# Two decode layers on one core: the last head of each pass loaded and worked off in another order

## The chip, the core and the metric

The kernel runs on one core of one Trainium2 chip. The metric is the device time of one execution in microseconds. Three runs of the kernel before gave 1331.91, 1332.23 and 1334.55 us, the median being 1332.23 us.

A profiled execution records when each engine worked. TensorE does the matrix products (PE in the rows, PEld its loads of stationary operands), VectorE is DVE, ScalarE is ACT, GpSimd is POOL, and SyncE (SP) issues the loads from HBM. "x16" counts trace records; each float32 product of the code is two records (two passes) in these rows.

## What is computed

Two layers, each of them attention and then a gated feed-forward part, run twice over the same weights and the same caches, for 2 batches and one new token each:

```python
def _A_ref(x, k_cache, v_cache, wq, wo):
    B, Sq, D = x.shape                 # 2, 1, 448
    H, Dh = 16, 256
    q = (x @ wq).reshape(B, Sq, H, Dh).transpose(0, 2, 1, 3)
    scores = jnp.einsum("bhqd,bhkd->bhqk", q, k_cache) * (Dh ** -0.5)   # 4096 keys
    o = jnp.einsum("bhqk,bhkd->bhqd", softmax(scores), v_cache)
    return o.transpose(0, 2, 1, 3).reshape(B, Sq, H * Dh) @ wo

def _B_ref(x, W_gate, W_up, W_down):   # 448 -> 1792 -> 448
    gate, up = x @ W_gate, x @ W_up
    return (gate * (gate > 0) * up) @ W_down

for _ in range(2):
    x = x + _A_ref(layernorm(x), A_k_cache, A_v_cache, A_wq, A_wo)
    x = x + _B_ref(layernorm(x), B_W_gate, B_W_up, B_W_down)
```

All of it is float32. Keys and values of one head and batch are 4 MB each, so that a pass over 32 of these pairs reads 256 MB.

## The kernel before, in words

**Units.** A unit is one pair of head and batch. A pass works through 32 units; the second pass takes them in the reverse order. `attention` keeps `n_u = 32`, and unit 31 is the last of a pass, unit 30 the one before it (both of one head).

**The arena.** All loads go into one big on-chip buffer, `arena`, of 27 places of 1 MB: six blocks of four places and three singles. `pending` is the list of all loads of the program in their order, written before any instruction. `pump()` takes loads from its front as long as there is a free place, and issues each on SP's queue; `release()` frees a place after its last use and calls `pump()` again. Keys or values of a unit are loaded as one piece of 4 MB, which needs a whole free block, or as four pieces of 1 MB. `grouped(keys, begin, end)` decides: the first `begin` and the last `end` pieces of a pass's list stay single. Each load on SP waits for the place's last reader, and, since eight semaphores are used in turn, for the landing of the load eight places earlier.

**Order of the loads.** For each unit its keys and then its values, with the next head's weights between; after unit 31 come seven pieces of the feed-forward input weights (`in`, 0.9 MB each) and four of the output weights (`out`). `keep` holds the pieces that the second pass will need first (22 pieces of keys and values and one head's weights): at the end of the first pass they stay in the arena and are not loaded again, which leaves four places for the eleven feed-forward pieces to pass through.

**A unit.** `score(u, c)` multiplies the query with a quarter of the keys into the PSUM banks `rawa` and `rawb` (L327). `score_copy` (DVE, L337) copies a bank to `found_s` or `row`, `score_turn` (L345) turns it by products with an identity. `softmax_max` and `softmax_exp` use DVE, POOL and ACT. `weigh(u, c)` (L382) multiplies the probabilities with a quarter of the values into `poa` or `pob`, two columns of probabilities against 512 columns, so that half of each result is used. `out_copy` (ACT, L395) and `out_add` (DVE, L398) bring the two useful halves together in `row`; `out_turn` (L406), `out_keep` (DVE, L415) and `project` (L245, through `add`) multiply with the output weights into `y`. These last three of unit u-1 stand between the scores of unit u. `query(u)` (L303, L306) makes the two queries of a head.

**Fillers.** `busy(n, half)` (L236) issues products whose result nobody reads, between the steps of units 30 and 31 and in the feed-forward part.

**Feed-forward.** `absorb()` (L250 to L261) takes the sum in `y` out and turns it, centred, into `xs`; `squares`, `deviation` (L281, L282) and `inverse` give one over the deviation; `again()` (L267) puts the residual back into `y`. `proj(0, ...)` and `proj(1, ...)` (L480) multiply `xs` with the `in` pieces, four and four parts, and release a piece after its last part. `hid` is formed (L504, L506), turned (L511, L516), and multiplied with 14 blocks of the `out` pieces (L245): even blocks go to partitions 0 and 32 of `y`, odd ones to 64 and 96. In the last feed-forward part only, the blocks after 6 all go to partitions 0 and 32, the upper half of `y` is copied to SBUF (L537) and added by two products (L541), so that one copy (L556) yields the output.

## Time and profile before

| | us |
|---|---|
| median of 3 runs | 1332.23 |
| the profiled execution | 1334.14 |
| its span, first to last instruction | 1332.3 |
| PE busy in the span | 1039.9 |
| DVE, ACT, POOL busy | 176.8, 91.7, 47.7 |
| read from HBM | 561.52 MB, 421 GB/s over the span |

Rows of the timeline read: start, duration, engine, line, operation, what it writes and reads, count, and in brackets the idle time of that engine just before and what ended it. Rows of the table by stretches read: stretch, its length, busy time of PE, PEld, DVE, ACT and POOL with counts, the granted share of the TensorE clock, the busy share of the DMA engines, and GB/s moved. A row on SP is the issue of a load, not the load.

### The profile page before, as it was taken

Reading aid. Unit: us, or ns where it says so; the run is one execution under the profiler, and the core shown is the slowest. Engines: PE = TensorE matmul, PEld = TensorE weight load, DVE = VectorE, ACT = ScalarE, POOL = GpSimd, SP = SyncE. Lnnn points to the kernel's source line nnn. Section 1 sums busy time; section 2 is a strip of 40 time slices with the busy share of each in tenths; the row PEclk is TensorE's granted clock in tenths of the full one; section 3 lists DMA queues with packets and bytes.
Section 4 is the critical chain, followed back from the end, with each engine's and each line's share of the span. In section 5 each row is a group of like instructions: output and inputs, shape, how many; then the busy total and the mean of one; then the engine's idle time right before and its main releaser. Section 6 shows DMA issues by size and latency. Waiting matters only on the chain.

```text
span 1332.3 us, 14966 instructions
## 1 busy us (share of the span) xinstructions
PE 1039.9 (78%) x6594; PEld 401.6 (30%) x6594; DVE 176.8 (13%) x522; ACT 91.7 (7%) x280; POOL 47.7 (4%) x134
## 2 busy tenths in 40 slices
PE   4876878787777877768889888787877777677888
PEld 2332222233232323223343333233232232222323
DVE  1111111111011111111101111111111111111110
ACT  1000000000000000000011000000000000000001
POOL 0000000000000000000000000000000000000000
PEclk9868667767677667776888887766667777777689
DMA  9999999999999999999989999999999999999997
GB/s 402 435 426 431 432 422 438 427 433 428 427 434 432 427 431 430 430 431 425 419 333 387 435 432 429 431 429 430 430 430 429 431 430 428 428 434 430 428 418 302
DMA packets 29598, 562.49 MB, mean 422 GB/s; under 512 B 3287, under 2 KB 3421, under 8 KB 10205
## 3 DMA queue, kind: packets, MB, share of 16 engines
q1 hardware_dynamic: 29524, 561.53, 98.8%
q8 instruction: 52, 0.85, 0.3%
q14 instruction: 14, 0.11, 0.0%
q10 hardware_dynamic: 8, 0.01, 0.0%
HBM read 561.52 MB, written 0.00 MB: 421 GB/s over the span
## 4 chain that ended last, share of the span: by engine, by line
PE 66%; DMA 15%; another core or an unknown queue 12%; DVE 3%; issue 2%; ACT 2%; POOL 1%; POOLq 0%; SPq 0%; ACTq 0%; DVEq 0%
PE pob L382 12%; PE poa L382 11%; PE rawa L327 11%; PE rawb L327 11%; PE small L345 11%; DMA arena<-in_k_cache_dram 7%; DMA arena<-in_v_cache_dram 5%; PE pq L303 3%; PE small L406 3%; DMA arena<-in_w_in_dram 2%; DVE row L337 2%; PE y L245 2%; PE pq L306 1%; ACT probs L362 1%
## 5 line engine op out<-in xcount | busy, mean ns | idle before, releaser
L327 PE MATMUL rawa<-arena,q 128*1 128x512 f32 x1024 | 172.1, 785 | 131.3 <-DMA arena<-in_k_cache_dram 130.9
L382 PE MATMUL pob<-arena,probs 128*2 128x512 f32 x1024 | 182.3, 866 | 53.6 <-DMA arena<-in_v_cache_dram 53.1
L382 PE MATMUL poa<-arena,probs 128*2 128x512 f32 x1024 | 177.5, 846 | 52.5 <-ACT probs L362 46.7
L327 PE MATMUL rawb<-arena,q 128*1 128x512 f32 x1024 | 169.7, 737 | 0.0
L345 PE MATMUL small<-ident,row 128*128 128x4 f32 x512 | 83.1, 286 | 30.3 <-DVE row L337 30.3
L345 PEld LDWEIGHTS small<-ident,row 128*128 128x128 f32 x512 | 77.5, 232 | 85.2 <-DVE row L337 85.2
L345 PEld LDWEIGHTS small<-ident,found_s 128*128 128x128 f32 x512 | 79.0, 236 | 71.4 <-issue 37.7
L327 PEld LDWEIGHTS rawa<-arena,q 128*1 128x1 f32 x1024 | 26.8, 91 | 241.3 <-issue 189.9
L345 PE MATMUL small<-ident,found_s 128*128 128x4 f32 x512 | 84.6, 289 | 0.0
L382 PEld LDWEIGHTS pob<-arena,probs 128*2 128x2 f32 x1024 | 30.6, 108 | 173.1 <-issue 170.1
L382 PEld LDWEIGHTS poa<-arena,probs 128*2 128x2 f32 x1024 | 29.6, 106 | 168.8 <-issue 117.2
L337 DVE COPY found_s<-rawa 128x512 f32<-128x512 f32 x64 | 44.2, 691 | 233.0 <-PE rawa L327 233.0
L337 DVE COPY row<-rawb 128x512 f32<-128x512 f32 x64 | 44.3, 691 | 228.6 <-PE rawb L327 228.6
L359 ACT ACTIVATE nm<-top,nsr 128x1 f32<-128x1 f32 x64 | 18.8, 294 | 733.4 <-POOL top L354 733.4
L406 PEld LDWEIGHTS small<-ones,row 128*128 128x128 f32 x256 | 42.9, 238 | 77.9 <-issue 53.8
L354 POOL PARTITION_ALL_REDUCE top<-mx x64 | 22.4, 351 | 1180.1 <-DVE mx L352 1180.1
L303 PE MATMUL pq<-xs,arena 128*128 128x2 f32 x384 | 57.9, 267 | 0.5 <-DVE xs L261 0.5
L303 PEld LDWEIGHTS pq<-xs,arena 128*128 128x128 f32 x384 | 54.3, 213 | 0.7 <-DVE xs L261 0.7
L406 PE MATMUL small<-ones,row 128*128 128x1 f32 x256 | 48.3, 293 | 0.5 <-DVE row L398 0.5
L398 DVE SCALAR_TENSOR_TENSOR row<-pob,ri,row 128x256 f32<-128x256 f32 x32 | 15.5, 484 | 230.9 <-ACT row L395 230.9
L398 DVE SCALAR_TENSOR_TENSOR row<-poa,ri,row 128x256 f32<-128x256 f32 x32 | 15.5, 484 | 168.2 <-ACT row L395 168.2
L395 ACT ACTIVATE row<-pob,ri 128x256 f32<-128x256 f32 x32 | 15.1, 473 | 250.8 <-PE pob L382 250.8
(80 smaller groups left out, 363.0 us busy)
## 6 DMA issues: line engine op xcount, KB each, us to landing
arena<-in_k_cache_dram SPq DMA_DIRECT2D x57, 4096.0 KB, 54.0
arena<-in_v_cache_dram SPq DMA_DIRECT2D x56, 4096.0 KB, 54.1
arena<-in_w_head_dram SPq DMA_DIRECT2D x31, 896.0 KB, 52.4
arena<-in_v_cache_dram SPq DMA_DIRECT2D x22, 1024.0 KB, 19.8
arena<-in_k_cache_dram SPq DMA_DIRECT2D x16, 1024.0 KB, 18.0
arena<-in_w_in_dram SPq DMA_DIRECT2D x14, 896.0 KB, 19.0
arena<-in_w_out_dram SPq DMA_DIRECT2D x4, 896.0 KB, 12.3
arena<-in_w_out_dram SPq DMA_DIRECT2D x3, 672.0 KB, 7.0
```

Of the source, the lines that this page charges most:

```text
L245: nc.tensor.matmul(y[at : at + B, : w_h.shape[1]], stat, w_h, **flags)
L303: nc.tensor.matmul(pq[:, j, :], w[:, at : at + P], xT[:, c, :], start=(c == 0), stop=False)
L306: nc.tensor.matmul(pq[:, j, :], w[:, FULL * DH : FULL * DH + P], xT[:, FULL + j, :], start=False, stop=True,)
L327: nc.tensor.matmul(raw[half][32 * g : 32 * g + 1, :], q_of[u][:, j, :], kt[:, g, :], start=(j == 0), stop=(j == 1),)
L337: nc.vector.tensor_copy(row if half else found_s, raw[half])
L345: nc.tensor.matmul(s_of[u][:, n : n + G], rows[:, e * P : (e + 1) * P], pick, start=True, stop=True,)
L354: nc.gpsimd.partition_all_reduce(mx_of[u], mx, P, RED.max)
L359: nc.scalar.activation(nm, mx_of.pop(u), AF.Copy, scale=nsr[:, b : b + 1])
L382: nc.tensor.matmul(po_of[u][32 * t : 32 * t + 2, :], p_of[u][:, n : n + 2], vt[:, 2 * t * DH : (2 * t + 2) * DH], start=(c == 0), stop=(c ...
L395: nc.scalar.activation(row[:, :DH], po_of[u][:, :DH], AF.Copy, scale=r_of[u][:, 0:1])
L398: nc.vector.scalar_tensor_tensor(row[:, :DH], po_of.pop(u)[:, DH:], r_of[u][:, 1:2], row[:, :DH], op0=ALU.mult, op1=ALU.add,)
L406: nc.tensor.matmul(pT_of[u][:, c : c + 1], row[:, c * P : (c + 1) * P], ones, start=True, stop=True,)
```

## The change

Units 30 and 31, the one head worked last in each of the two passes, are loaded as keys 30, keys 31, values 30, values 31. Only the last four pieces of a pass's list stay single (`ENDS` 4 instead of 12), so that keys 31 and values 30 are now one piece of 4 MB each. The scores of unit 31 come before the values of unit 30. The fillers between the scores of units 30 and 31 are gone; two stand behind each of the middle two quarters of `weigh(31)`. For unit 31, `weigh` uses one column of probabilities against 256 columns, so that `out_copy` alone gives the result and `out_add` is skipped. `again()` moves: in attention between the two halves of the first query, in the feed-forward part behind the first part of `proj(1)`. The deviation moves behind the first quarter of the scores, and behind the second part of `proj(1)`. In the last feed-forward part the blocks go to both halves of `y` up to block 10, the upper half is copied after that, added before block 13, and the filler there is gone.

```diff
-ENDS = 12
+ENDS = 4
...
-        for u, unit in enumerate(order):
+        for u, unit in enumerate(order[:-2]):
             found.append(("k", unit, 0))
-            if u % 2 and u + 1 < len(order):
+            if u % 2:
                 found.append(("h", order[u + 1][0], 0))
             found.append(("v", unit, 0))
-        return found
+        return found + [(kind, unit, 0) for kind in "kv" for unit in order[-2:]]
...
             for j in range(2):
+                if j and u == 0:
+                    again()
                 for c in range(FULL):
...
-        def first_query():
-
-            total = squares()
-            query(0)
+        def spread(total):
+
             deviation(total)
             nc.scalar.activation(nsr[:, :1], eps_t, AF.Exp)
+            inverse()
+            nc.vector.tensor_scalar_mul(sr, rstd, SCALE)
+            nc.vector.tensor_scalar_mul(nsr, rstd, -SCALE)
...
-            if u >= n_u - 2:
-                busy(1, u % 2)
...
-            for t in range(CT // 2):
+            for t in range(CT if u == n_u - 1 else 0):
+                n = c * CT + t
+                nc.tensor.matmul(
+                    po_of[u][32 * (t % 4) : 32 * (t % 4) + 1, :DH],
+                    p_of[u][:, n : n + 1],
+                    vt[:, t * DH : (t + 1) * DH],
+                    start=(c == 0 and t < 4),
+                    stop=(c == NC - 1 and t >= 4),
+                )
+            for t in range(CT // 2 if u < n_u - 1 else 0):
...
-            if u >= n_u - 2 and c < NC - 1:
-                busy(1, (u + 1) % 2)
+            if u == n_u - 1 and 0 < c < NC - 1:
+                busy(2, (u + 1) % 2)
...
         def out_add(u):
+            if u == n_u - 1:
+                return
...
             if u == n_u - 1:
-                busy(1, 0)
+                busy(2, 0)
...
+        for u in range(n_u - 1):
+            scores(u)
+            if u % 2:
+                query(u + 1)
+            if u < n_u - 2:
+                outputs(u)
+        u = n_u - 1
+        for c in range(NC):
+            score(u, c)
+        score_copy(u, 0)
+        score_copy(u, 1)
+        score_turn(u, 0)
+        score_turn(u, 1)
+        softmax_max(u)
+        softmax_exp(u)
+        outputs(u - 1)
+        out_turn(u - 1)
+        out_keep(u - 1)
+        outputs(u)
+        busy(1, 0)
+        out_turn(u)
+        out_keep(u)
+        project(u)
...
-                if half and n < 3:
+                if half and n == 0:
+                    again()
+                if half and n == 1:
+                    spread()
+                if half and 0 < n < 3:
                     busy(1, 0)
...
+                if last and k == 13:
+                    for half in range(2):
+                        n = D - DH if half else DH
+                        nc.tensor.matmul(
+                            y[32 * half : 32 * half + B, :n],
+                            ident[64:, 64 + 32 * half : 64 + 32 * half + B],
+                            yrow[64:, :n], start=False, stop=False,
+                        )
                 add(
-                    0 if last and k > 6 else k % 2, stat[k], w_k,
-                    start=(k == 1), stop=(k in ((5, 13) if last else (12, 13))),
+                    0 if last and k > 10 else k % 2, stat[k], w_k,
+                    start=(k == 1), stop=(k in ((9, 13) if last else (12, 13))),
                 )
             release("out", "", j)
-            if last and j == 1:
+            if last and j == 2:
                 nc.scalar.activation(yrow[64:], y[64:], AF.Copy)
...
-            if j < 3 or not last:
+            if j < 2 or not last:
                 busy(1, 0)
```

Below, the order of the instructions at three places, as the built programs have it (nothing on times is in it). First SP's loads at the end of the first pass, before; a row is a run of equal loads, 8192 columns being a piece of 4 MB and 2048 one of 1 MB:

```order
L131 DMA arena<-in_k_cache_dram 128x8192
L131 DMA arena<-in_v_cache_dram 128x2048 x4
L131 DMA arena<-in_k_cache_dram 128x2048 x4
L131 DMA arena<-in_v_cache_dram 128x2048 x4
L131 DMA arena<-in_w_in_dram 128x1792 x7
```

and with the change:

```order
L131 DMA arena<-in_k_cache_dram 128x8192 x2
L131 DMA arena<-in_v_cache_dram 128x8192
L131 DMA arena<-in_v_cache_dram 128x2048 x4
L131 DMA arena<-in_w_in_dram 128x1792 x7
L131 DMA arena<-in_w_out_dram 128x1792
```

Keys 31 stand ahead of values 30 now, and eight single pieces have become two of 4 MB. Second, TensorE from the last quarter of the values of unit 30 (`poa`) into the scores of unit 31, before:

```order
L382 MATMUL poa<-arena,probs 2x512 x4
L327 MATMUL rawa<-arena,q 1x512 x4
L236 MATMUL pob<-ident 2x256
L327 MATMUL rawa<-arena,q 1x512 x4
L236 MATMUL pob<-ident 2x256
L406 MATMUL small<-ones,row 128x1 x2
L327 MATMUL rawb<-arena,q 1x512 x4
L236 MATMUL pob<-ident 2x256
L345 MATMUL small<-ident,found_s 128x4 x4
L327 MATMUL rawb<-arena,q 1x512 x4
L236 MATMUL pob<-ident 2x256
L345 MATMUL small<-ident,row 128x4 x4
```

and with the change, from the scores of unit 31 to its last values (`pob`):

```order
L330 MATMUL rawa<-arena,q 1x512 x8
L330 MATMUL rawb<-arena,q 1x512 x8
L346 MATMUL small<-ident,found_s 128x4 x4
L346 MATMUL small<-ident,row 128x4 x4
L392 MATMUL poa<-arena,probs 2x512 x16
L418 MATMUL small<-ones,row 128x1 x2
L383 MATMUL pob<-arena,probs 1x256 x16
L236 MATMUL poa<-ident 2x256 x2
L383 MATMUL pob<-arena,probs 1x256 x8
L236 MATMUL poa<-ident 2x256 x2
L383 MATMUL pob<-arena,probs 1x256 x8
L236 MATMUL poa<-ident 2x256
```

The scores and turns of unit 31 have moved ahead of all values, without fillers. Third, TensorE near the end of the program, before, from block 6 of the output weights to block 7; "waits" names what an instruction waits for (DMAHW a load, Activation an instruction of ACT):

```order
L245 MATMUL y<-arena,near 2x256
L245 MATMUL y<-arena,near 2x192
L236 MATMUL poa<-ident 2x256
L245 MATMUL y<-arena,near 2x256 [waits DMAHW3_49,Activation_49]
L245 MATMUL y<-arena,near 2x192
```

and with the change, from block 10 to block 13:

```order
L245 MATMUL y<-arena,near 2x256
L245 MATMUL y<-arena,near 2x192
L245 MATMUL y<-arena,near 2x256 [waits DMAHW0_49,Activation_49]
L245 MATMUL y<-arena,near 2x192
L245 MATMUL y<-arena,near 2x256
L245 MATMUL y<-arena,near 2x192
L572 MATMUL y<-found_s,ident 2x256
L572 MATMUL y<-found_s,ident 2x192
L245 MATMUL y<-arena,near 2x256 [waits DMAHW1_49]
L245 MATMUL y<-arena,near 2x192
```

Block 11 (the third row) waits for the copy of the upper half on ACT; before, this wait stood at block 7, behind a filler. The two products that add the copy stand ahead of block 13 now, and ahead of block 11 before.

49 lines of the change are left out of this document (18 added, 31 removed).

## The prediction

> **What bounds the kernel now.** I read the page first, then the table of stretches around the middle and the end, then the timeline there.
>
> ```profile
> span 1332.3 us, 14966 instructions
> DMA  9999999999999999999989999999999999999997
> GB/s 402 435 426 431 432 422 438 427 433 428 427 434 432 427 431 430 430 431 425 419 333 387 435 432 429 431 429 430 430 430 429 431 430 428 428 434 430 428 418 302
> ```
>
> The loads set the time: the DMA engines are busy in every slice, near 430 GB/s, save in two places, slices 21 and 22 (333 and 387) and the last one (302). Only there can an unchanged volume end sooner. The middle in stretches of 5 us:
>
> ```profile
> 660.00:665.00 5.00, 4.36 (x33) 1.95 (x33) 0.94 (x4) 0.76 (x3) 0.73 (x2) 1.00 1.00 417
> 665.00:670.00 5.00, 4.48 (x33) 1.52 (x35) 0.64 (x2) 0.47 (x1) 0.00 (x0) 1.00 0.92 380
> 670.00:675.00 5.00, 4.55 (x30) 2.12 (x34) 0.50 (x3) 1.76 (x3) 0.00 (x0) 0.68 0.33 137
> 675.00:680.00 5.00, 5.00 (x38) 1.53 (x31) 0.06 (x1) 0.35 (x2) 0.00 (x0) 0.64 0.85 285
> 680.00:685.00 5.00, 3.55 (x34) 0.98 (x30) 0.43 (x3) 0.34 (x1) 0.00 (x0) 1.00 1.00 391
> ...
> 700.00:705.00 5.00, 5.00 (x34) 2.15 (x26) 1.03 (x3) 1.28 (x2) 0.00 (x0) 0.75 0.69 242
> ```
>
> Against 417 GB/s the four stretches from 665 to 685 lose 5 x (37 + 280 + 132 + 26) / 417 = 5.7 us of loading, and 700 to 705 another 2.1. Who holds the loads up there, the timeline and SP's waits tell:
>
> ```profile
> 645.27 0.33 SPq L131 DMA_DIRECT2D arena<-in_v_cache_dram  x1
> DMA to landing us min/median/max: 19.8/19.8/19.8
> 666.96 1.02 PE L382 MATMUL pob<-arena,probs 128*2 128x512 f32 x5
> 668.58 0.48 DVE L398 SCALAR_TENSOR_TENSOR row<-pob,ri,row 128x256 f32<-128x256 f32 x1 [4.53 <-ACT row L395]
> 669.12 0.61 PE L406 MATMUL small<-ones,row 128*128 128x1 f32 x4 [0.27 <-DVE row L398]
> 672.82 6.05 PE L480 MATMUL rawa<-arena,xs 128*32 128x448 f32 x32 [0.27 <-DVE xs L261]
> 674.60 0.33 SPq L131 DMA_DIRECT2D arena<-in_w_in_dram  x1
> SPq L131 <- PE rawa L480: 9.5, 3, 7.3
> 702.21 4.27 SPq L131 DMA_DIRECT2D arena<-in_k_cache_dram  x4
> ```
>
> The last values land at 645.27 + 19.8 = 665.07. Four feed-forward pieces follow and fill the four free places; the fifth is issued only at 674.60, when the first part of `proj(0)`, begun at 672.82, has given a place back (SP waited up to 7.3 us for L480). So between 665 and 675 the chain from the last values to `proj(0)` bounds, and TensorE is late in it: it ends the last values at 667.98, 2.9 us after their landing. At 702.21 SP waits in the same way for the first keys of the second pass.
>
> At the end of the second pass the same lateness costs nothing:
>
> ```profile
> 1310.85 3.21 PE L480 MATMUL rawa<-arena,xs 128*32 128x448 f32 x32 [0.27 <-DVE xs L261]
> 1319.39 0.96 PE L480 MATMUL rawb<-arena,xs 128*32 128x448 f32 x8 [0.82 <-DMA arena<-in_w_in_dram]
> 1322.51 1.09 PE L245 MATMUL y<-arena,near 128*2 128x192 f32 x16
> 1325.44 1.38 PEld L245 LDWEIGHTS y<-arena,near 128*2 128x2 f32 x16 [0.62 <-ACT found_s L537]
> 1325.44 1.89 PE L245 MATMUL y<-arena,near 128*2 128x256 f32 x16
> 1329.72 0.38 ACT L556 ACTIVATE found_s<-y 34x256 f32<-34x256 f32 x1 [4.33 <-PE y L245]
> ```
>
> `proj(1)` waits for its last piece until 1319.39, so the loads bound up to there; behind it stand 10.3 us of TensorE and small steps up to the copy at 1329.72. That piece's landing, and these 10.3 us, are what the change can move at the end.
>
> **The change part by part.** *Fewer pieces.* The issues of pieces of one size follow each other at the rhythm in which earlier ones land:
>
> ```profile
> 604.01 0.33 SPq L131 DMA_DIRECT2D arena<-in_v_cache_dram  x1
> 613.72 0.33 SPq L131 DMA_DIRECT2D arena<-in_k_cache_dram  x1
> 642.79 0.33 SPq L131 DMA_DIRECT2D arena<-in_v_cache_dram  x1
> ```
>
> 4 MB take 613.72 - 604.01 = 9.71 us, 1 MB takes 645.27 - 642.79 = 2.48, so four singles cost 9.92. Two groups of four become one piece each: -0.2 x 2 in each pass, **-0.8** in both, if all of it is on the path (bounds -0.8 and 0).
>
> *The last head in the new order.* With keys 31 loaded ahead of values 30, its scores can be done before its values are there. The scores of units without fillers, at half the clock (594, 635) and at the full one (614), and the page's row on the pieces of 4 MB, which land 54 us after their issue:
>
> ```profile
> 594.37 3.59 PE L327 MATMUL rawa<-arena,q 128*1 128x512 f32 x16 [3.55 <-DMA arena<-in_k_cache_dram]
> 605.15 1.87 PE L345 MATMUL small<-ident,row 128*128 128x4 f32 x8
> 614.59 1.89 PE L327 MATMUL rawa<-arena,q 128*1 128x512 f32 x16
> 635.43 1.88 PE L327 MATMUL rawa<-arena,q 128*1 128x512 f32 x8 [3.61 <-DMA arena<-in_k_cache_dram]
> arena<-in_k_cache_dram SPq DMA_DIRECT2D x57, 4096.0 KB, 54.0
> ```
>
> Scores of unit 30 from 635.43, as slow as those from 594.37 to 607.02 (12.6 us): 648.1. Scores of unit 31 follow at once, 2 x 3.6 us slow or 2 x 1.9 fast; as they are dense I take the middle, 5.4, and 2 us of turns (1.87 was a slow one): 655.5. Values 30 have landed then, two pieces of 9.7 us behind keys 30: 635.3 + 19.4 = 654.7; issued 54 us ahead, they do not dry the queue. Their four quarters of 8 passes take 2 x 1.9: 659.3. TensorE's next instruction, the turn of unit 30, now waits for out_copy and out_add, with all values of unit 31 queued behind it: 1.1 us from the end of the values to the turn (667.98 to 669.12) and 0.6 of the turn: 661.0. Two quarters, fillers, a quarter, fillers: 3 x 0.9 + 4 x 0.38 = 4.2: 665.2. The last quarter, landed at 664.7, takes 1.1 (row 1322.51: 16 passes of this width in four column groups): 666.3, against 667.98, so 1.7 sooner; with all scores slow, 0; with all fast, only the landing bounds and it is 2.2. Skipping out_add takes its 0.48 and a handover of 0.05 more off. So `proj(0)` starts 1.7 + 0.5 = 2.2 us sooner, between 0.5 and 2.7. It also runs faster if the clock is full: its 32 passes took 6.05 us here and 3.21 in the second pass, so that the first part, a quarter, gives its place back 0.7 sooner. The fifth piece is then issued 2.9 us sooner and all loads up to the keys of the second pass with it; what is late next are those keys, at 702.21. A gain beyond this is open: at 674.60 the engines had run nearly empty, and the loads came back at 285 and 391 GB/s; if the queue never runs dry, up to 5 x (132 + 26) / 417 = 1.9 more goes. I take a quarter of that, -0.5; of it all 0.2 is the earlier landing counted above: **-3.2**, bounds -0.5 and -4.8.
>
> *`again` and the deviation.* In the second pass's first query, `again` now stands in front of the second half of the query, whose copy the first scores wait for; the deviation leaves that place. TensorE works through all of it anyway:
>
> ```profile
> 699.09 0.16 DVE L311 COPY q<-pq 128x4 f32<-128x4 f32 x1 [3.19 <-PE pq L306]
> 699.40 0.59 PE L267 MATMUL y<-found_s,halves 128*2 128x256 f32 x2
> ```
>
> Before, the deviation and L267 covered the copy of the query (699.09, 0.16 us); now that copy and its handovers are bare, and the deviation delays the second quarter of keys. The issue at 702.21 comes some 0.25 later: **+0.25** (0 to +0.6). In the feed-forward part `again` replaces a filler of its own length in a stretch that waits for loads (row 1319.39), at no cost; if that wait is gone, 0.9 us.
>
> *The last blocks.* Blocks 7 to 10 now use both halves of `y`: 1.09 us as in the row at 1322.51 in place of 1.89, -0.8. One filler goes, -0.4. The copy of the upper half ran beside a filler, though the load row at 1325.44 waited 0.62 for it; now block 11 waits for it bare, with blocks 11 to 13, the two products and the last copy queued behind: +0.5. **-0.7** (bounds -0.2 and -1.3). The last piece has landed by then:
>
> ```profile
> arena<-in_w_out_dram SPq DMA_DIRECT2D x1, 224.0 KB, 14.7
> 1312.25 0.33 SPq L131 DMA_DIRECT2D arena<-in_w_out_dram  x1
> ```
>
> It lands at 1326.95; block 13 comes at about 1328.2.
>
> **Sum.** -0.8 - 3.2 + 0.25 - 0.7 = -4.45; the profiled execution took 1334.14 (1.84 around the span), so 1329.7. It is 1.9 us above the median of 1332.23; I read the difference as the clock in the middle, below, whose 0.7 us are then no gain for the faster runs: 1332.23 - 3.75 = 1328.5. I take **1328.8**, nearer to the second, since the measure is a median.
>
> **Rivals.** *The clock falls in the last head, and the kernel is slower.* What a stretch of little work for TensorE can do to its clock shows in three stretches of 3.4 us:
>
> ```profile
> 668.40:671.80 3.40, 2.70 (x23) 1.42 (x20) 0.64 (x2) 1.27 (x4) 0.00 (x0) 0.99 0.68 283
> 671.80:675.20 3.40, 3.13 (x20) 1.38 (x24) 0.50 (x3) 0.63 (x1) 0.00 (x0) 0.50 0.17 66
> 1306.60:1310.10 3.50, 2.79 (x22) 1.45 (x21) 0.65 (x2) 1.37 (x4) 0.00 (x0) 1.00 1.00 414
> ```
>
> A stretch of short products at 668.40 is followed by half the clock at 671.80; nearly the same one at 1306.60 was not. If values 30 and 31 fall into the half clock in both passes, eight quarters cost 0.9 more each and four fillers 0.4: 8.8 us, so that the last values end 7 later than now and `proj(0)` starts 6.5 later. At the end `proj(0)` would start at 1317, and its last part, with 1.5 us for each of the seven before it, would come up to 8 us behind 1319.39; I take half. Together 6.5 + 4 - 1.3 of the other terms: 1343. It decides from a granted clock of 0.5 in most of 655 to 666. Against it: the scores of unit 31 are 3.8 us and more of dense products just ahead. The Trainium skill, "TensorE: Matmul & The Clock Gate", section "Why this matters for your kernels", asks for no gap of over about 3 us without products, else the clock halves. By that rule no fall is due in the changed order, where I find gaps up to 2 us, and the sum above would stand; but the trace differs from it, since the clock fell at 671.80 with TensorE busy for 2.70 of 3.40 us. Chance 0.08.
>
> *The gain stops at half.* TensorE is late again, all scores being slow, and only out_add and half of the rest are won: -0.8 - 1.0 + 0.25 - 0.7 = -2.25, hence 1331.9, or 1330.5 from the median: 1331.0. For it speaks that the scores of unit 30 start at half the clock (635.43); against it, that those of unit 31 find all their keys landed and leave no pause. Chance 0.25.
>
> *More.* The queue never runs dry and the second gap (242 GB/s) shrinks too, as the first query meets a full clock: -4.8 and -1 with the other terms of -1.3: 1327.0. Chance 0.1.
>
> *The change doesn't do what it says:* a piece of 4 MB needs a whole free block; keys 31 or values 30 may be issued late and the queue run dry, up to 9.7 us a piece. The 54 us leave room for several such delays, so that a third of one piece in each pass is the most that I see, 6.5 us, less 4.5: 1336. Chance 0.02.
>
> **How the numbers follow.** The forecast has 0.55, with its own range 1327.1 to 1330.6. What a measurement can tell from no change is about 0.2%, 2.7 us: faster is below 1329.57. Faster: three quarters of the forecast (0.41), all of "more" (0.10) and a little of "half" (0.03): 0.54. Slower: 0.09, the clock and nearly all of the late pieces. Same: the rest, 0.37. The range for 8 in 10 reaches down to "more" and up past half the gain: 1326.6 to 1332.3.
>
> **What would show it.** Right: the fifth `in` piece issued less than 8 us after the last values land (9.5 now), the last values ended within 1.5 us of their landing, the two slow slices at over 333 and 387 GB/s, a full clock for the last head's values. The end: block 11 waiting 0.4 to 0.6 us for ACT. Wrong: the loads' rate between 665 and 685 unchanged, although `proj(0)` starts sooner; or a clock of 0.5 with the values.

## The result, and the profile after

The changed kernel took 1330.39 us (median of 12 runs, 1328.27 to 1334.29), the kernel before beside it 1332.72 (12 runs, 1331.36 to 1334.75). The ratio is 0.9982, with a 95% interval of 0.9974 to 0.9991: 2.3 us faster by the medians, where the forecast was 3.4 below the older median of 1332.23. Measured a second time (in the experiments below) the ratio was 0.9989, 0.9980 to 0.9998. The ratios here and below go by all runs, so that they can differ from the medians by a microsecond. The profiled execution of the change took 1331.07, that of before 1334.14.

The changed kernel's page, the same rows as shown of before:

```profile
span 1329.3 us, 14932 instructions
...
DMA  9999999999999999999999999999999999999997
GB/s 402 435 425 434 428 425 435 432 426 430 430 432 430 432 426 433 430 430 430 420 371 377 435 430 431 430 427 432 430 429 431 431 427 432 427 432 431 430 421 301
```

Slices 21 and 22 stood at 333 and 387 GB/s and stand at 371 and 377: the gap in the middle is smaller, not gone, and still the only one beside the end. The same stretches of the middle (columns: from and to, length, busy time and count of PE, PEld, DVE, ACT, POOL, granted clock, DMA share, GB/s):

```profile
660.00:665.00 5.00, 3.88 (x58) 1.76 (x54) 0.94 (x4) 0.47 (x1) 0.00 (x0) 1.00 1.01 418
665.00:670.00 5.00, 4.57 (x50) 1.95 (x46) 0.16 (x1) 0.65 (x2) 0.00 (x0) 1.00 0.89 366
670.00:675.00 5.00, 4.25 (x39) 1.89 (x41) 0.51 (x3) 0.30 (x2) 0.00 (x0) 1.00 0.49 155
675.00:680.00 5.00, 3.97 (x36) 1.14 (x32) 0.49 (x3) 2.09 (x3) 0.00 (x0) 1.00 0.99 404
680.00:685.00 5.00, 3.73 (x32) 1.53 (x24) 0.80 (x2) 0.00 (x0) 0.00 (x0) 1.00 1.03 431
...
700.00:705.00 5.00, 3.90 (x35) 1.56 (x28) 1.45 (x3) 0.97 (x2) 0.00 (x0) 0.97 0.92 372
```

Before, 665 to 685 went at 380, 137, 285 and 391 GB/s; now at 366, 155, 404 and 431. The hole is as deep and one stretch shorter. The clock is 1.00 where it was 0.68 and 0.64, so this comparison doesn't tell the change from the clock: an execution with the old head and a full clock, in the experiments below, goes at 378, 152, 417 and 420 in the same stretches. The timeline of the change, by the names of the prediction:

```profile
645.09 3.10 PE L330 MATMUL rawa<-arena,q 128*1 128x512 f32 x16 [1.87 <-DMA arena<-in_k_cache_dram]
654.90 5.77 PE L392 MATMUL poa<-arena,probs 128*2 128x512 f32 x32 [2.62 <-DMA arena<-in_v_cache_dram]
661.80 0.61 PE L418 MATMUL small<-ones,row 128*128 128x1 f32 x4 [1.12 <-DVE row L410]
666.44 1.24 PE L383 MATMUL pob<-arena,probs 128*1 128x256 f32 x13
671.86 2.46 PE L511 MATMUL rawa<-arena,xs 128*32 128x448 f32 x24 [0.27 <-DVE xs L261]
672.88 1.83 SPq L131 DMA_DIRECT2D arena<-in_w_in_dram  x3
681.94 0.96 PE L511 MATMUL rawb<-arena,xs 128*32 128x448 f32 x8 [0.82 <-DMA arena<-in_w_in_dram]
698.71 5.53 SPq L131 DMA_DIRECT2D arena<-in_k_cache_dram  x4
```

`proj(0)` starts at 671.86 (672.82 before), the fifth piece is issued at 672.88 (674.60), the keys of the second pass at 698.71 (702.21). But the last values, landed at 664.7, end only at 667.68, as late as before. The reason stands two rows above their row (666.44), in the row of values 30: in this execution TensorE was early, not late. It waited 2.62 us for values 30, which come as one piece now, and then took 5.77 us for 32 passes that were counted at 3.8. Its clock:

```profile
649.00:652.40 3.40, 3.28 (x32) 1.97 (x20) 0.77 (x2) 0.00 (x0) 0.00 (x0) 0.99 0.85 361
652.40:655.80 3.40, 0.90 (x8) 0.23 (x12) 0.41 (x3) 0.76 (x3) 0.76 (x2) 0.51 1.00 417
655.80:659.30 3.50, 3.50 (x24) 0.64 (x20) 0.00 (x0) 0.00 (x0) 0.00 (x0) 0.50 1.02 425
```

Half a clock from 652.5 to 659.3. The wait had begun only 0.2 us before the cut, at 652.28, and the stretch ahead of it has PE busy for 3.28 of 3.40 us; 1.9 us of that are the turns of unit 31, products of four columns.

At the end, the change's timeline and two stretches:

```profile
1315.38 0.96 PE L511 MATMUL rawb<-arena,xs 128*32 128x448 f32 x8 [0.81 <-DMA arena<-in_w_in_dram]
1324.36 0.52 PEld L245 LDWEIGHTS y<-arena,near 128*2 128x2 f32 x8 [1.05 <-ACT found_s L583]
1324.36 1.02 PE L245 MATMUL y<-arena,near 128*2 128x256 f32 x8 [0.55 <-ACT found_s L583]
1326.49 0.38 ACT L594 ACTIVATE found_s<-y 34x256 f32<-34x256 f32 x1 [2.17 <-PE y L245]
```

```profile
1314.70:1318.10 3.40, 2.29 (x20) 1.26 (x20) 0.62 (x1) 0.00 (x0) 0.00 (x0) 1.00 0.94 383
1318.10:1321.50 3.40, 3.40 (x31) 1.21 (x30) 0.18 (x1) 0.00 (x0) 0.00 (x0) 0.50 0.54 222
```

Block 11 waits 0.55 us for ACT, as forecast (0.4 to 0.6). From the last part of `proj(1)` to the end of the last copy it is 11.5 us (1315.38 to 1326.87), against 10.7 before (1319.39 to 1330.10): the blocks of 1318 to 1321 ran at half the clock.

Profile against profile, then, the lead of the change over before was 3.0 us at the last part of `proj(1)` in the middle, 3.5 at the first keys of the second pass, 4.0 at the last part at the end, and 3.2 at the last copy. The prediction's terms add up to 3.6, 3.35, 3.75 and 4.45 at these four places. But the profile of before is of a long execution, 1.4 us above the median of the 12 runs, and the experiments show how much of this lead is owed to that.

### The profile page after: what moved, and what is told of

Same layout as the page of the kernel before. It is cut to its first block, busy times and chain, and to the rows that moved or that the text cites. A ratio compares the mean times of both kernels' runs of the same rounds, so it can differ in the third digit from the quotient of the medians.

```text
span 1329.3 us, 14932 instructions
## 1 busy us (share of the span) xinstructions
PE 1027.0 (77%) x6588; PEld 404.1 (30%) x6588; DVE 174.3 (13%) x520; ACT 92.1 (7%) x280; POOL 47.7 (4%) x134
## 4 chain that ended last, share of the span: by engine, by line
PE 62%; DMA 17%; another core or an unknown queue 13%; DVE 3%; ACT 1%; issue 1%; POOL 1%; SPq 0%; POOLq 0%; ACTq 0%
PE poa L392 11%; PE pob L392 11%; PE rawa L330 10%; PE small L346 10%; PE rawb L330 10%; DMA arena<-in_v_cache_dram 7%; DMA arena<-in_k_cache_dram 7%; PE pq L305 3%; PE small L418 3%; DVE row L338 2%; DMA arena<-in_w_in_dram 2%; PE y L245 1%; PE pq L308 1%; ACT probs L363 1%
## 5 line engine op out<-in xcount | busy, mean ns | idle before, releaser
L330 PE MATMUL rawa<-arena,q 128*1 128x512 f32 x1024 | 168.4, 788 | 140.9 <-DMA arena<-in_k_cache_dram 140.4
L392 PE MATMUL pob<-arena,probs 128*2 128x512 f32 x960 | 171.4, 879 | 39.4 <-DMA arena<-in_v_cache_dram 39.4
L305 PE MATMUL pq<-xs,arena 128*128 128x2 f32 x384 | 65.6, 287 | 0.5 <-DVE xs L261 0.5
L305 PEld LDWEIGHTS pq<-xs,arena 128*128 128x128 f32 x384 | 62.4, 241 | 2.4 <-issue 1.7
## 6 DMA issues: line engine op xcount, KB each, us to landing
arena<-in_k_cache_dram SPq DMA_DIRECT2D x8, 1024.0 KB, 10.7
```

The costliest lines, as they stand in the source:

```text
L305: nc.tensor.matmul(pq[:, j, :], w[:, at : at + P], xT[:, c, :], start=(c == 0), stop=False)
L330: nc.tensor.matmul(raw[half][32 * g : 32 * g + 1, :], q_of[u][:, j, :], kt[:, g, :], start=(j == 0), stop=(j == 1),)
L392: nc.tensor.matmul(po_of[u][32 * t : 32 * t + 2, :], p_of[u][:, n : n + 2], vt[:, 2 * t * DH : (2 * t + 2) * DH], start=(c == 0), stop=(c ...
```

## The experiments

All were timed in five rounds beside the kernel before. The theory to test: the head's order brings most of the gain, along a chain from the last values to `proj(0)`. Its rivals: the gain is cut down or made by the clock, and by where the loads themselves set the time.

**The three parts alone.** The head in the new order with the rest as before:

```
-                if j and u == 0:
-                    again()
...
-                if half and n == 0:
-                    again()
-                if half and n == 1:
-                    spread()
-                if half and 0 < n < 3:
+                if half and n < 3:
...
-            if last and j == 2:
+            if last and j == 1:
                 nc.scalar.activation(yrow[64:], y[64:], AF.Copy)
```

> The last head's new order, pieces and single copy alone; again, the deviation and the last blocks as before. Theory (the gain is the chain from the last values to proj(0) in the middle, and the queue not running dry): most of the gain is here, -2 to -3 us against before, with the fifth input piece issued 8 to 8.5 us after the last values land (9.5 before, 8.2 in the change) and the tail behind the last input piece as before, 10.3 us. Rival (the place of again and of the deviation let the places go sooner): -0.5 or less here.

Measured: 1331.20 us, ratio 0.9988 (0.9978 to 0.9998). Its timeline:

```profile
648.09 3.54 PE L328 MATMUL rawa<-arena,q 128*1 128x512 f32 x16
655.15 3.62 PE L390 MATMUL poa<-arena,probs 128*2 128x512 f32 x32
659.87 0.61 PE L416 MATMUL small<-ones,row 128*128 128x1 f32 x4 [1.11 <-DVE row L408]
664.78 1.04 PE L381 MATMUL pob<-arena,probs 128*1 128x256 f32 x16
669.99 2.46 PE L513 MATMUL rawa<-arena,xs 128*32 128x448 f32 x24 [0.27 <-DVE xs L261]
671.01 2.67 SPq L131 DMA_DIRECT2D arena<-in_w_in_dram  x3
674.51 0.97 PE L513 MATMUL rawa<-arena,xs 128*32 128x448 f32 x8 [2.05 <-DMA arena<-in_w_in_dram]
681.12 1.09 PE L513 MATMUL rawb<-arena,xs 128*32 128x448 f32 x8
```

In this execution the head ran as the prediction had laid it out: scores of unit 31 from 648.09 (counted: 648.1), values 30 from 655.15 (655.5), the turn at 659.87 (660.4, the end of its 0.6 at 661.0), the last values ended at 665.82 (666.3), `proj(0)` at 669.99 (670.6). The clock was full from 651.4 to 675.3, and then half for 3.4 us:

```profile
651.40:658.30 6.90, 6.90 (x68) 2.88 (x60) 1.87 (x5) 0.76 (x3) 0.76 (x2) 1.00 0.97 405
675.00:680.00 5.00, 5.00 (x37) 1.74 (x32) 0.49 (x3) 0.70 (x2) 0.00 (x0) 0.66 1.00 373
```

Yet the median gain is 1.3 us, against the 4.0 counted for the head and the pieces; it lies between what the theory asked (2 to 3) and what the rival asked (0.5 or less).

The last blocks alone, on the kernel before:

```
-                    0 if last and k > 6 else k % 2, stat[k], w_k,
-                    start=(k == 1), stop=(k in ((5, 13) if last else (12, 13))),
+                    0 if last and k > 10 else k % 2, stat[k], w_k,
+                    start=(k == 1), stop=(k in ((9, 13) if last else (12, 13))),
...
-            if j < 3 or not last:
+            if j < 2 or not last:
                 busy(1, 0)
```

> The last blocks alone, on the kernel before. Theory (0.7 us shorter at the full clock, longer where the clock falls in it): -0.7 us against before if the clock stays full behind the last input piece, as it did before; the wait for the copy ahead of block 11 is 0.5 us. Rival (the new tail itself is longer, since block 11 waits bare): +0.3 or more at the full clock.

Measured: 1332.06 us, ratio 0.9996 (0.9985 to 1.0006). And `again` and the deviation alone in their new places:

```
-        first_query()
-        again()
-        inverse()
...
+            if u == 0:
+                spread(total)
...
+                if half and n == 0:
+                    again()
+                if half and n == 1:
+                    spread()
```

> again and the deviation in their new places alone, on the kernel before. Theory (they stand where TensorE waits for loads anyway): within 0.5 us of before; the first keys of the second pass are asked for 9.1 to 9.9 us after the last output piece lands (9.7 before). Rival (the earlier release of the fourth input piece keeps the queue from running dry): -1 to -1.5 us, with the loads between 675 and 685 us above 350 GB/s.

Measured: 1331.48 us, ratio 0.9994 (0.9985 to 1.0004). Neither can be told from no change. (The sign named for the rival of `again`, loads above 350 GB/s between 675 and 685, is there: 426 and 422. But the last blocks alone, which leave `again` in its place, have 417 and 420 there too, so that it comes with the full clock and not with `again`.) Both keep the old head, and both profiles show what the profile of before did not: the old head followed by a full clock. The last blocks alone, then `again` alone:

```profile
672.17 3.21 PE L480 MATMUL rawa<-arena,xs 128*32 128x448 f32 x32 [0.27 <-DVE xs L261]
673.19 1.83 SPq L131 DMA_DIRECT2D arena<-in_w_in_dram  x3
679.93 0.96 PE L480 MATMUL rawb<-arena,xs 128*32 128x448 f32 x8 [0.81 <-DMA arena<-in_w_in_dram]
682.12 0.96 PE L480 MATMUL rawb<-arena,xs 128*32 128x448 f32 x8 [0.82 <-DMA arena<-in_w_in_dram]
```

```profile
671.62 3.32 PE L482 MATMUL rawa<-arena,xs 128*32 128x448 f32 x32 [0.27 <-DVE xs L261]
672.64 1.98 SPq L131 DMA_DIRECT2D arena<-in_w_in_dram  x3
681.88 0.96 PE L482 MATMUL rawb<-arena,xs 128*32 128x448 f32 x8 [0.81 <-DMA arena<-in_w_in_dram]
```

With the clock full, the old head issues the fifth piece at 673.2 and 672.6, and the last part of `proj(1)` starts at 682.1 and 681.9. Before's profile had 684.91: most of that lateness belonged to that execution, not to the kernel. And there is a floor under this place. Pieces land 2.19 us apart when the queue is full (679.93 to 682.12), so seven of them behind values that landed at 664.7 can't be there before 664.7 + 7 x 2.18 = 680.0. The old head at a full clock is 2.0 us above that floor; the new head is 1.1 above it (681.12). Of the 1.6 to 2.2 us that it gains at the fifth piece, 0.8 to 1.0 is left at the last.

Head alone shows where a part of it goes. The old head at a full clock runs through all four parts of `proj(0)` without a wait (3.21 us from 672.17). The new one begins 2.2 us sooner and then waits 2.05 us for the fourth piece, so that this part begins at 674.51, about where three quarters of 3.21 us put it with the old head (674.6). The landing of that piece now sets the time there, and not the chain. In head alone, in the change's second profile and in the version with four pieces (both below) half the clock follows that wait, from 674.7 to 675.3 on for 3.4 us; in two others with a wait of 1.9 us it doesn't.

**One for one, or not?** The change with 20 more filler passes (about 4.4 us) between the last values and the turn of the last head, in the first pass:

```
-        busy(1, 0)
+        busy(11 if after else 1, 0)
         out_turn(u)
```

> The change with 20 more passes of filler (0.22 us each at full clock, 4.4 in all) between the last values and the turn of the last head, in the first pass alone. Theory A (from the last values to the first part of the feed-forward part the chain bounds, one for one): the fifth feed-forward piece is issued 4.4 us later than in the change's run beside it, everything behind it too, and the time is 4 to 4.5 us longer, about 1334.8. Rival B (dense fillers keep the clock full, and the loads come back without a gap in their shares, so that a part is won back): 2 to 3 us longer, about 1333. Rival C (the stretch isn't on the path): under 1 us longer.

and, beside it, the changed kernel once more:

> The changed kernel once more, unaltered, so that its time is known twice and stands beside the two others. If the first measurement is right: 2.3 us below the kernel before, within 0.9. If the forecast is right and the first measurement was high: 3.4 or more below. The profile shows again whether the clock falls during values 30 (half clock between 650 and 660), or in another place.

Measured: 1335.72 us (1333.05 to 1336.65, 11 runs) against 1330.71 for the change (1329.70 to 1333.77, 11 runs), 5.0 longer by the medians; their ratios to the kernel before are 1.0018 (1.0009 to 1.0027) and 0.9989 (0.9980 to 0.9998), which makes it 3.9. The late kernel, then the change:

```profile
674.75 1.08 SPq L131 DMA_DIRECT2D arena<-in_w_in_dram  x2
683.85 0.96 PE L511 MATMUL rawb<-arena,xs 128*32 128x448 f32 x8 [0.81 <-DMA arena<-in_w_in_dram]
702.91 5.85 SPq L131 DMA_DIRECT2D arena<-in_k_cache_dram  x4
```

```profile
670.84 2.73 SPq L131 DMA_DIRECT2D arena<-in_w_in_dram  x3
680.93 0.96 PE L511 MATMUL rawb<-arena,xs 128*32 128x448 f32 x8
698.31 6.25 SPq L131 DMA_DIRECT2D arena<-in_k_cache_dram  x4
```

Theory A holds in the direction of late: the chain sets the end, and the 4.4 us are paid in full as far as can be told, 3.9 to 5.0 with an uncertainty of about 1. The path there is not even: 3.9 later at the fifth piece, 2.9 at the last part (1 us disappears above the floor), 4.6 at the first keys. A part of what comes back behind the last part is the clock: the first half of the query took 1.44 us in the late kernel and 0.83 in the change. So "later" costs about all of it, and "sooner" runs into the floor. Rival C falls, and the 2 to 3 us of rival B lie at the lower edge of what was measured or below it. In this execution of the change the clock did not fall in the head (values 30 took 3.61 us from 654.77, the last values ended at 665.65); it fell behind the wait for the fourth piece, at 674.7. The 1.9 us of this measurement (1330.71 against 1332.64; 1.5 by the ratio) and the 2.3 of the first are one figure within their intervals.

**Does the fall of the clock in the last head cost anything?** Two ways of keeping it out, and one of making up for it. Values 30 in four pieces again, so that TensorE finds them sooner:

```
-ENDS = 4
+ENDS = 8
```

> The change with values 30 in four single pieces again (keys 31 stay one piece). Theory (in the change TensorE idles 2.6 us for the whole of values 30, its clock falls, and so it ends the last values 3 us late): TensorE starts values 30 some 2 us sooner at the full clock, ends the last values within 2 us of their landing, and proj(0) starts about 1 us sooner than in the change; 1329.5, 0.9 below the change. Rival (the bigger pieces are what was won): 0.4 slower than the change, 1330.8.

Measured: 1329.59 us, ratio 0.9979 (0.9971 to 0.9987). The last quarter of the values then waits for nothing but its landing:

```profile
654.77 3.62 PE L392 MATMUL poa<-arena,probs 128*2 128x512 f32 x32
664.93 1.04 PE L383 MATMUL pob<-arena,probs 128*1 128x256 f32 x16 [0.42 <-DMA arena<-in_v_cache_dram]
```

Fillers in the pause ahead of values 30:

```
         softmax_max(u)
+        busy(4, 1)
         softmax_exp(u)
         outputs(u - 1)
```

> The change, with four fillers between the turns of unit 31 and the values of unit 30. Theory (in executions in which TensorE is early, it idles for values 30, its clock falls and it ends the last values late): values 30 run at the full clock in every execution, the last values end 1.1 to 2 us after their landing (3.0 in the change's profile), 1329.8. Rival (the four fillers stand in the path when TensorE is not early): slower than the change by up to 1, 1331.

Measured: 1330.49 us, ratio 0.9987 (0.9978 to 0.9996), although the profile shows what was wanted: values 30 in 3.62 us from 654.94, the last values ended at 665.83. The time lies between the theory's and the rival's, and doesn't differ from the change's.

And the other way round, the fillers behind the quarters of the last values left out, so that a late TensorE can catch up:

```
-            if u == n_u - 1 and 0 < c < NC - 1:
-                busy(2, (u + 1) % 2)
```

> The change without the two times two fillers behind the quarters of values 31. Theory (they stand ahead of the last quarter and cost time when TensorE is late): the last values end within 1.5 us of their landing also after an idle wait, 0.5 to 1 below the change, 1329.6. Rival (they hold the clock): the clock falls in the last values and in proj(0), 1331.5.

Measured: 1329.83 us, ratio 0.9979 (0.9970 to 0.9988). Here the clock fell ahead of values 30 just as in the change's first profile, and the lack of fillers won the time back:

```profile
654.86 5.89 PE L392 MATMUL poa<-arena,probs 128*2 128x512 f32 x32 [2.61 <-DMA arena<-in_v_cache_dram]
662.40 3.63 PE L383 MATMUL pob<-arena,probs 128*1 128x256 f32 x64
```

The values end at 666.03, against 667.68 with the fillers: when TensorE is late, the two groups of fillers are 1.65 us of delay. What they may be good for shows when both edits are put together:

```
-ENDS = 4
+ENDS = 8
...
-            if u == n_u - 1 and 0 < c < NC - 1:
-                busy(2, (u + 1) % 2)
```

> The change with two things taken back: values 30 come as four single pieces again, and the fillers behind the quarters of the last values are gone. Theory A (the fall of the clock during values 30, with the fillers behind it, costs the change up to 1.6 us in some executions, and each of the two edits takes it away by itself): the last values end within 1.4 us of their landing, and the time is 1.0 to 1.5 us below the change measured beside it, 1329.0 or so, no better than either edit alone. Rival B (the two costs add): 1.5 to 2.5 us below the change, about 1328. Rival C (where the clock falls next swallows it): the same as the change within 0.5 us, with the half clock somewhere between 668 and 685 in the profile.

Measured: 1330.24 us, ratio 0.9990 (0.9978 to 1.0002), with a spread of 7.7 us (1328.71 to 1336.37), against 4.4 and 3.1 for either edit alone, each from 11 or 12 runs. The profiled execution was the longest, and its stretches say why:

```profile
657.50:660.90 3.40, 2.26 (x36) 1.15 (x36) 0.94 (x4) 0.01 (x1) 0.00 (x0) 1.00 1.01 421
660.90:664.30 3.40, 1.41 (x24) 0.31 (x16) 0.00 (x0) 0.00 (x0) 0.00 (x0) 1.00 1.01 417
664.30:667.70 3.40, 2.51 (x18) 0.65 (x18) 0.00 (x0) 0.47 (x1) 0.00 (x0) 0.50 1.03 426
671.10:674.50 3.40, 3.13 (x14) 1.98 (x16) 0.51 (x3) 0.00 (x0) 0.00 (x0) 0.50 0.27 108
```

Each quarter was done at once and the engine waited for the next, busy for 1.41 of 3.40 us; the clock was halved from 664.3 to 677.9, `proj(0)` began at 673.90 and took 5.19 us. Rival C comes nearest: the time of the change within half a microsecond, and the half clock in this place. The two edits, 0.6 to 1.1 us below the change each by the medians, don't add as far as this can tell. In the execution shown they leave the engine idle where the fillers had kept it at work; whether that is so in the usual execution, one profile doesn't say.

The four-piece version once more, as the candidate to beat both:

> The change with values 30 as four single pieces, once more, unaltered. The change itself stood at 0.9982 and 0.9989 in its two measurements. Theory A (values that come in quarters keep the last head's values at the full clock in nearly every execution): 0.9975 to 0.9983, with most executions within 1.5 us of each other, and the profile has a full clock from 651 to 668. Rival B (the first measurement of it was lucky): 0.9984 to 0.999, not to be told from the change.

Measured: 1330.46 us, ratio 0.9977 (0.9967 to 0.9987). The ratio is that of theory A. It came out at 0.9979 and 0.9977, the change at 0.9982 and 0.9989: the version beats the kernel before, and perhaps the change by half a microsecond, which the intervals don't settle. The full clock that theory A wanted to see was not there, though: the second quarter of the last values took 1.89 us at 659.84, the last values ended at 667.25, and this execution took 1334.17.

**Filling the feed-forward part.** On the four-piece version, one filler behind the third part of `proj(0)`, two in place of one behind the second and third parts of `proj(1)`, and two in place of one behind its last:

```
                 if half and 0 < n < 3:
+                    busy(2, 0)
+                if not half and n == 2:
                     busy(1, 0)
...
-        busy(1, 0)
+        busy(2, 0)
```

> Values 30 in four pieces, and fillers where the feed-forward part waits: one behind the third part of proj(0), two instead of one behind the second and third parts of proj(1), two instead of one behind its last. Theory (what the change loses is the clock falling in the feed-forward parts): full clock from the first part of proj(0) to the last copy, at most 10.2 us from the last input part to that copy (11.5 in the change), fewer slow executions, 1328.8. Rival (the clock there is no cost in most executions): as without these fillers, 1329.6.

Measured: 1330.04 us, ratio 0.9984 (0.9975 to 0.9992). Then more of them in `absorb` and in the first query:

```
+        busy(1, 0)
...
+        busy(1, 0)
...
                 if j and u == 0:
                     again()
+                    busy(2, 0)
...
+            if u == 0:
+                busy(1, 0)
```

> As the last, with fillers also while the sum is taken out (one before and one behind the turning products), two in the first query behind again, one behind the query. Theory (the second gap of the loads, about 700 us, is the half clock of the query and the first scores): the first scores run at the full clock and the first keys are asked for 1 to 1.5 us sooner after the last output piece (9.1 in the change), 1327.7. Rival (fillers in the path cost what the clock gives): within 0.5 of the last kernel or slower.

Measured: 1330.55 us, ratio 0.9993 (0.9984 to 1.0002). In both profiles the clock is full from `proj(0)` to the end of the feed-forward part, the last part is followed by the end of the last copy within 10.1 us as the theory asked, and the first keys are issued at 696.96 and 697.39, the earliest of all; the medians are no better. Both profiles are of executions faster than the median of their kernel (1328.99 and 1329.89), so they don't show what the usual execution loses.

The middle of twelve profiled executions, from the rows of their timelines (us in the execution):

| kernel | values end | `proj(0)` | fifth piece | last part | first keys | span |
|---|---|---|---|---|---|---|
| before | 667.98 | 672.82 | 674.60 | 684.91 | 702.21 | 1332.3 |
| last blocks alone | 667.64 | 672.17 | 673.19 | 682.12 | 698.42 | 1329.5 |
| `again` alone | 667.09 | 671.62 | 672.64 | 681.88 | 698.08 | 1328.7 |
| change | 667.68 | 671.86 | 672.88 | 681.94 | 698.71 | 1329.3 |
| change, again | 665.65 | 669.82 | 670.84 | 680.93 | 698.31 | 1328.4 |
| head alone | 665.82 | 669.99 | 671.01 | 681.12 | 698.57 | 1328.9 |
| four pieces | 665.97 | 670.14 | 671.16 | 681.38 | 698.35 | 1328.3 |
| four pieces, again | 667.25 | 671.44 | 672.46 | 682.73 | 701.12 | 1332.4 |
| filled ahead of values 30 | 665.83 | 670.00 | 671.02 | 681.11 | 697.92 | 1328.7 |
| no fillers | 666.03 | 670.20 | 671.22 | 680.94 | 697.83 | 1327.7 |
| both of these | 667.08 | 673.90 | 675.68 | 685.80 | 701.79 | 1334.3 |
| late turn | 665.49 | 673.73 | 674.75 | 683.85 | 702.91 | 1334.9 |

Two things stand in it. From the issue of the first keys to the end of the span it is 629.9 to 632.5 us in every one: the executions differ mainly in the middle. And the first keys come at 697.8 to 698.7 in eight of them, with the old head (698.08 and 698.42) and the new (697.83 to 698.71). The other four had a long middle: before and "both of these" with a clock of 0.5 around `proj(0)`, four pieces again with one from 679.5 to 689.7, late turn by its added fillers. So the lead of the new head, 1.6 to 2.2 us at the fifth piece and about 1 at the last part, is not to be seen any more at the first keys, between executions without a long middle. What the medians show, about 2 us, no pair of these profiles shows as a lead that is carried along the chain. The loads say the same. From 665 to 685 only two of the six with the new head, no fillers and filled ahead of values 30, move more than the two with the old (372 and 378 GB/s against 342 and 358; the other four 339 to 359), and from 685 to 700 these two move less (333 and 336 against 380 and 369), so that by 700 their lead is used up. The two with the old head are of executions somewhat faster than their kernels' medians (1331.37 against 1332.06, 1330.46 against 1331.48). That the old head has a long middle more often would fit; one profile of each run can't show it. The three medians of the parts alone, -1.3, -0.5 and -1.0, add up to -2.8 against -2.3 and -1.9 for the whole, each good to about 1.3.

## Why the prediction was right, and where it was off

- **What bounds the kernel: right.** The loads, save in the middle and at the end; 4.4 us put into the chain there cost 3.9 to 5.0.
- **Fewer pieces, -0.8: not resolved.** The last values of the first pass landed at 664.7 in the change and at 664.9 with the four singles kept, so that 0.2 in a pass is possible; the medians don't show it.
- **The chain of the last head, 2.2 us to `proj(0)`: right in size where the clock was as assumed.** Head alone it ran within 0.5 us of the count, and `proj(0)` started at 669.8 to 670.2 in six of the ten profiled executions with the new head (those with added fillers in the feed-forward part included, late turn not), against 671.6 and 672.2 with the old head at full clock: 1.4 to 2.4. In the change's own first profile it was 1.0 only, the values having run at half the clock. The step that was missing there: values 30 as one piece make an early TensorE wait, and the fillers then delay a TensorE that has become late.
- **"and all loads up to the keys of the second pass with it": the step that failed.** The term of -3.2 was mis-sized at its last link. Against the old head at a full clock, 1.4 to 2.4 us are won at the start of `proj(0)` and 0.5 to 1.2 are left at the last part of `proj(1)` (680.93 to 681.38 against 681.88 and 682.12), since the loads have a floor at 680.0 that the old head missed by only 2.0. At the first keys of the second pass nothing is left (697.83 to 698.71 against 698.08 and 698.42). Why the medians are 2 us apart all the same stays open. The 0.7 for a faster `proj(0)` was a gain over one execution alone, and the 0.5 for a queue that never runs dry did not come in the change's profile: 155 GB/s still stand at 670 to 675, as with the old head at a full clock (152). In head alone it is 303 there, and what was won is lost behind, with 373 and 315 up to 685.
- **Which execution the sum is made against: half right.** The profile of before stood 1.4 us above the median of its 12 runs, and the reason was named correctly, the clock in the middle; but 0.7 was taken off for it. Its last part at 684.91, against 682 in two others with that head, was worth 2.8. The sum of -4.45 less the whole distance to the median, 1.4 to 1.9, would have given -2.5 to -3.0, next to the -2.3 measured; but as the -3.2 in it was too large, that nearness proves nothing. The time of 1330.39 lies 0.2 us inside the forecast's own range (1327.1 to 1330.6), and the second measurement, 1330.71, 0.1 outside: that the first came out inside is luck. Both lie in the range for 8 in 10 (1326.6 to 1332.3).
- **`again` and the deviation, +0.25: not resolved.** Alone they gave -1.0 with an interval that holds zero. From the last part of `proj(1)` to the first keys it is 16.3 to 17.5 us with the old places (before, last blocks alone, head alone) and 16.0 to 19.1 with the new ones (the other nine of the table), by the clock there; 0.25 can't be seen in that.
- **The last blocks, -0.7: right at full clock.** From the last part to the end of the last copy it was 10.71 to 10.73 with the old blocks (three executions), and 10.06 to 10.25 with the new in six executions, but 11.4 to 11.5 in five others, the change's profile among them, whose clock fell at the blocks. None of the three with the old blocks shows that fall; whether the edit makes it likelier stays open, as the cut comes from a stretch ahead of the edited blocks.
- **The rivals.** "The gain stops at half" gave 1331.0 (the middle of 1331.9 and 1330.0; the 1330.5 in it is a slip, since 1332.23 - 2.25 = 1329.98), and 1330.4 and 1330.7 were measured, nearer to it than to the forecast's 1328.8; but its mechanism, all scores slow and TensorE late from the start, is not what the profiles show. "The clock falls in the last head" did occur, in the change's profile, at a price of about 2 us in the first pass (667.68 against 665.65 to 665.82), not 7, as only values 30 were hit and not values 31. For the end "half of up to 8" was wrong: `proj(0)` of the second pass started at 1306.67, and nothing was lost.
- **The signs named.** Fifth piece less than 8 us after the landing of the last values: 8.2 in the change's profile, 6.3 in the head alone and in four pieces. Values ended within 1.5 us of it: 3.0, and 1.1 in these two. Both slow slices higher: only the first. Block 11: yes. The sign of being wrong, the loads' rate between 665 and 685 unchanged: not against the profile of before, but against the old head at a full clock (378, 152, 417, 420) the change has 366, 155, 404 and 431, and so the sign is there. The other, half the clock with the values, came in the change's profile with values 30.

## What to carry to other kernels

Before a gain is taken over along a chain, look for the floor under its far end: here the pieces' own rhythm (seven at 2.18 us behind the last values) allowed at most 2 us, whatever the chain won. A single profile that stands above the median of its kernel is a poor base where the clock moves in steps: compare two or three executions before a stall is priced. Fillers can protect the clock when the engine is early and cost their length when it is late; taking them out or feeding the engine sooner each did no harm here, and both together won nothing more.

## What was not expected of the hardware

The granted clock fell behind stretches in which TensorE was hardly idle: at 652.5 behind 3.28 busy us of 3.40, and in before at 671.8 behind 2.70 of 3.40. In the first 1.9 us, in the second some 1.2 us of the busy time were products of one to four columns. It did not fall at 661.0 in the four-piece version:

```profile
657.60:661.00 3.40, 2.29 (x32) 1.04 (x28) 0.94 (x4) 0.47 (x1) 0.00 (x0) 1.00 1.00 414
661.00:664.40 3.40, 3.40 (x44) 1.34 (x33) 0.00 (x0) 0.00 (x0) 0.00 (x0) 1.00 0.99 411
```

There PE was busy for 2.29 us only, but with 24 passes of 512 and 256 columns among them. So it looks as if the columns streamed count, and not the busy time.

No run tried it by itself, but all 2668 stretches at the full clock in the 14 profiles can be counted (left out: the first 20 us; a pass counts a quarter of its columns for each 32 partitions that it writes to, which is a choice). Behind a stretch of up to 700 columns the clock was half in 683 of 686, behind one of 1600 or more it stayed full in 1217 of 1222, and between these both happen. The stretch ahead of 652.5 has 1088, that of before 662, that of the four pieces 1796. The best bound on the columns, 1100, sorts 2523 of the stretches rightly, the best bound on PE's busy time 2165. An exception is the stretch of before at 1306.6: 662 columns, and the clock stayed full. Why TensorE's wait for the fourth piece was followed by half the clock in some executions fits this too: 1008 columns in head alone, where it fell, and 2016 in no fillers, where it didn't.

The Trainium skill, "TensorE: Matmul & The Clock Gate", section "Why this matters for your kernels", asks for no gap of over about 3 us. At 652.5 the wait of 2.62 us begins 0.2 us ahead of the cut, and both falls come without a gap of that length, so that these traces show that keeping the rule is not enough. The stretches are some 3.4 us long and begin at other times in each execution (652.5, 664.3, 671.8), which fits the spread of several us between the runs of one kernel (1328.27 to 1334.29 for the change); that the spread comes from it was not shown.
